# Two more slots for converted weights, the last three inner blocks taken output by output, and the operand differences of the second MLP moved

## The chip, the cores and the metric

The kernel runs on one core of one Trainium2 chip. The metric is the device time of one execution in microseconds. The engines of the core are named as in the profile: PE (TensorE, matmuls; PEld is its weight load), DVE (VectorE), ACT (ScalarE), POOL (GpSimd) and SP (SyncE, which issues the DMAs here).

## The reference

Attention, then two MLPs on 1152 tokens (2 batches of 576) with 512 features. The parts that the change touches are the two MLPs:

```python
def _moe_ref(x, w_in, w_out):                 # first MLP: 512 -> 2048 -> 512
    h = x @ w_in
    relu6 = np.clip(h + 3.0, 0.0, 6.0)
    g = h * relu6 / 6.0
    return g @ w_out

def _moe2_ref(x, domain_probs, w1, w2):       # second MLP: 4 experts, 512 -> 1024 -> 512
    p = domain_probs / (domain_probs.sum(-1, keepdims=True) + 1e-09)
    out = 0
    for e in range(4):
        h = np.maximum(x @ w1[e], 0.0)
        out += p[:, e:e + 1] * (h @ w2[e])
    return out
```

## The kernel before

All matmuls of the MLPs are three-term products: each float32 operand is a high part, which TensorE takes as it is, and a low part (the difference), and high x high, high x low and low x high are accumulated (`three`, L350, and `product`, L861). ACT makes a high part by a copy, DVE the low part by a subtraction.

**First MLP.** The weights come as 16 pieces of 128 x 1024 double-precision words: 8 of `w_in`, then 8 of `w_out`. The generator `converting` (L173) turns a piece into a high and a low half in steps: DVE masks (L219), DVE adds the low word (L229) and ACT prepares the next piece's scale (L195), DVE multiplies (L241, L250) and ACT copies the high half (L203), DVE subtracts the low half (L208). `convert(n)` takes n steps if more than two slots are free; `need` takes as many as are needed. A piece uses a slot for its source (`raw`), one for scratch (`temps`) and keeps one for the result. Slots of 8 KiB per partition come from pools: `slots` (11), `mlp1` (6) and, once the attention's result x is no longer needed, `more` (4), which lies where x was. The function `take` goes through a list of pools in order and takes the first that has a slot by the count kept while the program is written out.

The first product, `first` (L763), runs for 16 inner blocks f of 128 and 3 token groups c of 384; its result, gated, goes to `gate_of` slots, five blocks to a slot. The second product, `second` (L834), runs c by c, f by f: `split_gate` makes the pair h (high by ACT L787, low by DVE L788) two blocks ahead, and each h is multiplied with four pieces of weight, one for each of four outputs dt of 128 features, 12 matmuls in all (L354 to L356), accumulating in four PSUM banks. After f = 15 ACT evicts the four outputs to x2 (L853). The tile `h` has NF2 = 8 buffers. The order of TensorE is that of the program. DVE, ACT and POOL are ordered by a planner in this part, which simulates the program and lets an engine take, of what is ready, what stands first in the program.

**Second MLP.** The tokens are two halves (s = 0 and 1) of 576. The products follow a scheme that works on differences of blocks: `blocks_of_x2(s, xop)` takes the four blocks b[c, h] (c: features, h: half of the tokens) of x2, makes four differences on POOL (L278, called by `sub2`), and splits seven operands, named 11, T2, T1, T3, 21, 22, T4, each by an ACT copy (L284) and a DVE subtraction (L289). It is a generator, and one step is one operand. For s = 0 it runs during the last token group of the first MLP (`prepare_first`, two steps per block), with w1 and w2 of the first expert (`load_in`, `sum_in`, `prepare_in`, `prepare_out`; the four sums of a w1 part are on POOL, L407 and L278). For s = 1 it runs after the last token group. From there on DVE, ACT and POOL follow the program's order too. A round r has four `Unit2` of 42 products: `open` (12), `middle` (18) and `close` (12), with a unit's close after the next one's open. Close accumulates into the banks of middle, once DVE has read them (L407). Then nine token tiles go through `second2` (L1098 to L1100).

In round 0 two operands of s = 1 are split ahead of unit 1, three after it, and the rest after unit 2. The shares `pr` of the experts (L1120 to L1125) are computed before all that.

Of the kernel before, what the change touches and what calls it, by code (L numbers as in the profile page):

```python
# [80 lines left out]
NB = 6  # L81
NX = 2 * KD * NT // SLOT

# [27 lines left out]
def model(ctx: ExitStack, tc: tile.TileContext, qT, kT, v, dp, w_in, w_out, w1, w2, out):  # L114
# [45 lines left out]
    sources = [w_in[i].bitcast(I32) for i in range(NW)] + [w_out[i].bitcast(I32) for i in range(NW)]  # L160
    raw, wt = {}, {}
    loaded = [0]
    SHORT = ("more", "slots", "mlp1")
    LONG, FIRST = ("mlp1", "slots"), ("slots", "mlp1")

    def load_to(n):
        while loaded[0] <= min(n, len(sources) - 1):
# [109 lines left out]
    def sub2(out, a, b, eng=None):  # L277
        (eng or nc.gpsimd).tensor_tensor(out=out, in0=a, in1=b, op=ALU.subtract)  # L278
# [503 lines left out]
        )  # L782

    def split_gate(c, f):
        g = hp_.tile([P, 2, TC], F32R, tag="h", name="h", bufs=NF2)
        u = gate_of(c, f)
        nc.scalar.activation(out=g[:, 0, :], in_=u, func=AF.Copy)  # L787
        nc.vector.tensor_tensor(out=g[:, 1, :], in0=u, in1=r32(g[:, 0, :]), op=ALU.subtract)  # L788
        n = c * NF1 + f
        if n % PER == PER - 1 or n == NTC * NF1 - 1:  # L790
            give(g_slots.pop(n // PER))
        return g
# [14 lines left out]
    def blocks_of_x2(s, x):  # L807

        b = {}
        for c in (0, 1):  # L810
            t = x2_pair(s, c)[:, : 2 * PAIR].rearrange("p (k a n) -> p k a n", k=2, a=2)
            for h in (0, 1):
                b[c, h] = t[:, :, h]
        room = x2_pair(s, 0)[:, 2 * PAIR : 3 * PAIR].rearrange("p (k n) -> p k n", k=2)
        x = x.rearrange("p (b h k n) -> p b h k n", b=7, h=2, k=2)

        def put(at, of):
            return splits([(x[:, at, 0], x[:, at, 1], of)])

        yield from put(0, b[0, 0])  # L820
        sub2(b[0, 0], b[0, 1], b[0, 0])
        sub2(room, b[1, 1], b[0, 0])
        sub2(b[0, 1], b[1, 1], b[0, 1])
        yield from put(4, b[1, 0])
        sub2(b[1, 0], b[1, 0], room)
        yield from put(1, room)
        yield from put(2, b[0, 0])
        yield from put(3, b[0, 1])
        yield from put(5, b[1, 1])
        yield from put(6, b[1, 0])  # L830
        for c in (0, 1):
            give(x2_slots.pop((s, c)))

    def second(c, f, g, accs):  # L834
        n = NW + f // 2
        need(n)
        for dt in range(KD):
            c0 = (f % 2) * DM + dt * P
            three(
                accs[dt],  # L840
                wt[n],
                slice(c0, c0 + P),
                (g[:, 0, :], g[:, 1, :]),
                f == 0,
                f == NF1 - 1,
            )
        if f < NF1 - 1:
            return
        for dt in range(KD):
            for s, n0 in enumerate((0, PAIR)):  # L850
                lo, hi = max(c * TC, n0), min((c + 1) * TC, n0 + PAIR)
                if lo < hi:
                    nc.scalar.activation(  # L853
                        out=x2_at(s, dt)[:, lo - n0 : hi - n0],
                        in_=accs[dt][:, lo - c * TC : hi - c * TC],
                        func=AF.Copy,
                        scale=1.0 / UP**2,
                    )


    def product(ps, a, b, start, stop):  # L861
# [150 lines left out]
    psum.pop("pair").release()  # L1012
    psum["many"] = ctx.enter_context(tc.tile_pool(name="many", bufs=6, space=PSUM))
    att.release()
    hp_ = tc.alloc_tile_pool(name="hp", bufs=1, side="right")
    for f in range(NF1):
        for c in range(1 if f < EARLY else 0, NTC):
# [33 lines left out]
    for n, (c, f) in enumerate(gs):  # L1051
        if f == 0:
            accs = [bank(TC) for _ in range(KD)]
        if n + 2 < len(gs):
            ready.append(split_gate(*gs[n + 2]))
        second(c, f, ready.pop(0), accs)
        if c == 0:
            convert(2, 1)
        elif c == 1 and f == 3:
            for _ in conv:  # L1060
                pass
        elif c == 2 and f == 0:
            assert unused.pop("more") == NX
            pools.pop("more").release()
            work["sums"] = ctx.enter_context(
                tc.tile_pool(name="sums", bufs=1, reuse_waits="tile")
            )
            xops.append(work["sums"].tile([P, 28 * TB], F32R, name="xop0"))
            first_of = prepare_first()
        elif c == 2:  # L1070
            run(first_of, 2)
        if c == NTC - 1 and f % 2:
            done_with(NW + f // 2)
    assert unused.pop("mlp1") == NB
    for _ in first_of:
        pass
    hp_.release()
    pools.pop("mlp1").release()
    work["pool"] = tc.alloc_tile_pool(name="work", bufs=1, side="right", reuse_waits="tile")
    xops.append(work["pool"].tile([P, 28 * TB], F32R, name="xop1"))  # L1080
# [10 lines left out]
    def second2(r, t, h):  # L1091
# [24 lines left out]
    )  # L1116
    dps = work["pool"].tile([P, NTT, E], F32, name="dps")
    nc.sync.dma_start(out=dps, in_=dp)
    psum_ = work["pool"].tile([P, NTT], F32, name="psum_")
    nc.vector.tensor_reduce(out=psum_, in_=dps, op=ALU.add, axis=AX.X)  # L1120
    nc.vector.tensor_scalar(out=psum_, in0=psum_, scalar1=1e-9, scalar2=None, op0=ALU.add)
    prec = work["pool"].tile([P, NTT], F32, name="prec")
    nc.vector.reciprocal(out=prec, in_=psum_)
    pr = work["pool"].tile([P, NTT, E], F32, name="pr")
    nc.vector.tensor_tensor(  # L1125
        out=pr, in0=dps, in1=prec.unsqueeze(2).to_broadcast([P, NTT, E]), op=ALU.mult
    )
    load_in(1)
    for r in range(NR):
        h = [  # L1130
            work["pool"].tile([P, 2, 2, NT], F32R, tag="h", name="h", bufs=2) for _ in range(2)
        ]
        if r == 0:
            order, steps = [(0, 0), (1, 0), (0, 1), (1, 1)], blocks_of_x2(1, xops[1])
        else:
            order, steps = [(0, 0), (0, 1), (1, 0), (1, 1)], prepare_out(r, 1)
            load_in(r + 1)
        before = None
        run(steps, 2 if r == 0 else 0)
        for i, (n, p) in enumerate(order):  # L1140
            unit = Unit2(r, n, xops[p], h[n], p)
            unit.open()
            if before:
                before.close()
            unit.middle(before)
            before = unit
            run(steps, 3 if r == 0 else 1)
            if i == 1:
                for _ in steps:
                    pass  # L1150
                load_out(r + 1)
            if i == 2:
                sum_in(r + 1, 0)
        for t in range(NTT):
            second2(r, t, h)
            if t == 0:
                before.close()
                before.lows()
                for n in (0, 1):
                    drop(w_in2, (r, n))  # L1160
                steps = chain(prepare_in(r + 1, 0), prepare_in(r + 1, 1), prepare_out(r + 1, 0))
            run(steps, 2 if t % 2 else 1)
        for _ in steps:
            pass
        for q in (0, 1):
            drop(w_out2, (r, q))
# [46 lines left out]
```

## Time and profile before

| | us |
|---|---|
| median of 3 runs | 665.03 (663.31 to 666.17) |
| the profiled execution | 664.96 |
| its span, first to last instruction | 663.1 |
| PE busy | 646.5 (97%) |
| DVE busy | 419.1 (63%) |
| ACT busy | 251.7 (38%) |
| POOL busy | 102.3 (15%) |

The granted TensorE clock is 0.995 of full speed over the span. In the trace the first product of the first MLP ends near 175.5 us, its second product runs from there to 279.1, the second MLP (eight rounds) from there to the end. Each row of a timeline gives start and duration in us, engine, line, operation, what is written and read, and in brackets the idle time before it and what ended that. Consecutive rows of one line are merged ("x4"), with their union as the duration.

### The profile page before, as it was taken

How to read it: one execution, taken by the hardware profiler on the slowest of the kernel's cores; microseconds unless marked ns; L12 is line 12 of the kernel's file. 1: busy time of each engine (PE TensorE's matmuls, PEld its weight loads, DVE VectorE, ACT ScalarE, POOL GpSimd, SP SyncE). 2: the span in 40 equal slices, each digit the busy share in tenths (PEclk: the TensorE clock that was granted, in tenths of full speed). 3: DMA queues.
4: the chain of work that ended last, by engine and by line, in shares of the span. 5: the costliest groups of instructions: out<-in, count | busy, mean ns of one | idle time of the engine just before them, and what ended most of it. 6: DMA issues, size and time to landing. Idle time of an engine off the chain costs nothing.

```text
span 663.1 us, 11940 instructions
## 1 busy us (share of the span) xinstructions
PE 646.5 (97%) x4930; PEld 582.3 (88%) x4943; DVE 419.1 (63%) x825; ACT 251.7 (38%) x588; POOL 102.3 (15%) x146
## 2 busy tenths in 40 slices
PE   6989999999999999989999999999999999999997
PEld 3556899999998999988898898998998998988985
DVE  7466799942598229296575575665665665665742
ACT  2556666542475236243142232233232241331310
POOL 4653100000000035060120211201201201201000
PEclk8989999999999999999999999999999999999999
DMA  8933313300350013200120110110110210300012
GB/s 264 341 90 128 124 64 127 127 1 0 127 192 1 0 64 92 100 1 2 48 81 0 64 65 1 63 64 1 65 64 0 73 56 0 127 2 1 1 48 96
DMA packets 11860, 45.89 MB, mean 69 GB/s; under 512 B 1303, under 2 KB 3351, under 8 KB 7709
## 3 DMA queue, kind: packets, MB, share of 16 engines
q1 hardware_dynamic: 11804, 45.12, 20.1%
q8 instruction: 39, 0.64, 0.4%
q14 instruction: 17, 0.13, 0.1%
HBM read 42.76 MB, written 2.36 MB: 68 GB/s over the span
## 4 chain that ended last, share of the span: by engine, by line
PE 89%; DVE 8%; issue 1%; ACT 1%; POOL 0%; POOLq 0%; ACTq 0%
PE bank L865 25%; PE bank L1098 10%; PE bank L1100 10%; PE bank L1099 10%; PE bank L356 9%; PE bank L354 9%; PE bank L355 8%; PE pair L514 2%; PE pair L707 2%; DVE slot L229 1%; PE pair L428 1%; DVE slot L208 1%; PE pair L718 1%; DVE slot L250 1%; PE pair L687 1%
## 5 line engine op out<-in xcount | busy, mean ns | idle before, releaser
L865 PEld LDWEIGHTS bank<-xop,slot 128*128 128x128 f32 x1344 | 180.8, 188 | 3.8 <-DVE u L407 2.5
L865 PE MATMUL bank<-xop,slot 128*128 128x288 f32 x1344 | 182.1, 295 | 2.0 <-DVE u L407 2.0
L1098 PE MATMUL bank<-slot,h 128*128 128x512 f32 x288 | 113.4, 394 | 0.0
L1100 PE MATMUL bank<-slot,h 128*128 128x512 f32 x288 | 113.0, 392 | 0.0
L1099 PE MATMUL bank<-slot,h 128*128 128x512 f32 x288 | 111.9, 389 | 0.0
L1106 DVE SCALAR_TENSOR_TENSOR slot<-bank,pr,slot 128x512 f32<-128x512 f32 x63 | 47.3, 751 | 82.5 <-PE bank L1100 82.5
L407 POOL TENSOR_TENSOR st<-slot 128x256 f32<-128x256 f32 x16 | 13.2, 825 | 443.1 <-DMA slot<-in_w_dram 223.2
L356 PE MATMUL bank<-h,slot 128*128 128x384 f32 x192 | 65.0, 338 | 0.9 <-DVE slot L208 0.9
L354 PE MATMUL bank<-h,slot 128*128 128x384 f32 x192 | 64.8, 338 | 0.5 <-ACT slot L203 0.5
L1100 PEld LDWEIGHTS bank<-slot,h 128*128 128x128 f32 x288 | 54.1, 188 | 12.6
L355 PE MATMUL bank<-h,slot 128*128 128x384 f32 x192 | 64.6, 337 | 0.0
L1099 PEld LDWEIGHTS bank<-slot,h 128*128 128x128 f32 x288 | 54.1, 188 | 11.5
L1098 PEld LDWEIGHTS bank<-slot,h 128*128 128x128 f32 x288 | 54.1, 188 | 10.3
L354 PE MATMUL bank<-x,slot 128*128 128x384 f32 x188 | 63.1, 336 | 0.0
L356 PE MATMUL bank<-x,slot 128*128 128x384 f32 x188 | 62.9, 335 | 0.0
L355 PE MATMUL bank<-x,slot 128*128 128x384 f32 x188 | 62.9, 335 | 0.0
L407 DVE TENSOR_TENSOR u<-bank,u 128x288 f32<-128x288 f32 x96 | 43.6, 454 | 20.8 <-PE bank L865 20.5
L894 ACT ACTIVATE h<-c 128x288 fp32r<-128x288 f32 x64 | 27.9, 445 | 72.5 <-DVE c L407 72.5
L780 DVE SCALAR_TENSOR_TENSOR slot<-t,bank 128x384 f32<-128x384 f32 x47 | 25.8, 552 | 28.7 <-ACT t L779 28.4
L779 ACT ACTIVATE t<-bank,half__171 128x384 f32<-128x384 f32 x47 | 27.1, 581 | 41.9 <-PE bank L356 41.9
L284 ACT ACTIVATE slot<-st 128x512 fp32r<-128x512 f32 x32 | 19.2, 624 | 62.2 <-POOL st L278 62.2
L788 DVE TENSOR_TENSOR h<-slot,h 128x384 fp32r<-128x384 f32 x48 | 27.6, 584 | 22.2 <-ACT h L787 22.2
(113 smaller groups left out, 929.9 us busy)
## 6 DMA issues: line engine op xcount, KB each, us to landing
slot<-in_w_dram SPq DMA_DIRECT2D x16, 1024.0 KB, 4.8
slot<-in_w_in_dram SPq DMA_DIRECT2D x8, 1024.0 KB, 5.5
slot<-in_w_out_dram SPq DMA_DIRECT2D x8, 1024.0 KB, 4.8
slot<-in_v_dram SPq DMA_DIRECT2D x6, 512.0 KB, 9.1
out_dram<-slot SPq DMA_DIRECT2D x9, 256.0 KB, 2.0
slot<-in_kT_dram SPq DMA_DIRECT2D x3, 576.0 KB, 6.7
slot<-in_qT_dram SPq DMA_DIRECT2D x6, 288.0 KB, 6.1
slot<-in_kT_dram SPq DMA_DIRECT2D x2, 288.0 KB, 3.7
```

The source lines that it names most:

```text
L354: nc.tensor.matmul(ps, wh, xh, start=first, stop=False)
L355: nc.tensor.matmul(ps, wh, xl, start=False, stop=False)
L356: nc.tensor.matmul(ps, wl, xh, start=False, stop=last)
L407: eng.tensor_tensor(out=out, in0=a, in1=b, op=ALU.add)
L779: nc.scalar.activation(out=t, in_=ps, func=AF.Relu, bias=half_, scale=1.0 / (6.0 * UP))
L788: nc.vector.tensor_tensor(out=g[:, 1, :], in0=u, in1=r32(g[:, 0, :]), op=ALU.subtract)
L865: nc.tensor.matmul(ps, a[:, i, k], b[:, j, k], start=start and k == 0 and n == 0, stop=stop and k == 1 and n == 2, skip_group_check=True,)
L894: nc.scalar.activation(out=self.h[:, 0, i, j], in_=of, func=AF.Relu)
L1098: nc.tensor.matmul(ps, hh, w[:, 0], start=(f == 0), stop=False)
L1099: nc.tensor.matmul(ps, hh, w[:, 1], start=False, stop=False)
L1100: nc.tensor.matmul(ps, hl, w[:, 0], start=False, stop=(f == NF - 1))
L1106: nc.vector.scalar_tensor_tensor(out=to, in0=ps, scalar=share, in1=to, op0=ALU.mult, op1=ALU.add)
```

## The change

- A pool `late` of NL = 2 slots is opened when the attention's room is free, next to `h`, whose buffers go from 8 to NH = 4. The lists of `take` name it: sources, scratch and first gated blocks may go there, later weights and loads prefer it.
- In the last token group, the last LAST = 3 inner blocks are multiplied output by output: for each dt the nine matmuls of f = 13, 14 and 15, then its eviction (`put_x2`).
- `blocks_of_x2` starts with three of the four differences, into places of their own (t1, t2) so that none of them overwrites a block that is still to be split, and the order of the operands is 11, 21, 22, T1, T2, T3, T4.
- In round 0, three operands are split ahead of unit 1, then one after each open and one after each middle of units 1 and 2. The shares are computed after unit 2 (`shares`).

```diff
+NL = 2
+NH = 4
+LAST = 3
-    SHORT = ("more", "slots", "mlp1")
-    LONG, FIRST = ("mlp1", "slots"), ("slots", "mlp1")
+    SHORT = ("more", "slots", "late", "mlp1")
+    LONG, FIRST = ("late", "mlp1", "slots"), ("slots", "late", "mlp1")
...
-        g = hp_.tile([P, 2, TC], F32R, tag="h", name="h", bufs=NF2)
+        g = hp_.tile([P, 2, TC], F32R, tag="h", name="h", bufs=NH)
...
-        yield from put(0, b[0, 0])
-        sub2(b[0, 0], b[0, 1], b[0, 0])
-        sub2(room, b[1, 1], b[0, 0])
-        sub2(b[0, 1], b[1, 1], b[0, 1])
-        yield from put(4, b[1, 0])
-        sub2(b[1, 0], b[1, 0], room)
-        yield from put(1, room)
-        yield from put(2, b[0, 0])
-        yield from put(3, b[0, 1])
-        yield from put(5, b[1, 1])
+        sub2(t1, b[0, 1], b[0, 0])
+        sub2(t2, b[1, 1], t1)
+        sub2(b[0, 1], b[1, 1], b[0, 1])
+        yield from put(0, b[0, 0])
+        yield from put(4, b[1, 0])
+        sub2(b[1, 0], b[1, 0], t2)
+        yield from put(5, b[1, 1])
+        yield from put(2, t1)
+        yield from put(1, t2)
+        yield from put(3, b[0, 1])
         yield from put(6, b[1, 0])
...
-    def second(c, f, g, accs):
+    def second(c, fs, gs, accs):
+        for f in fs:
+            need(NW + f // 2)
         for dt in range(KD):
+            for f, g in zip(fs, gs):
+                c0 = (f % 2) * DM + dt * P
+                three(accs[dt], wt[NW + f // 2], ...)
+            if f == NF1 - 1:
+                put_x2(c, dt, accs[dt])
...
+    pools["late"] = tc.alloc_tile_pool(name="late", bufs=NL, side="right")
+    unused["late"] = NL
...
-        second(c, f, ready.pop(0), accs)
+        if c < NTC - 1 or f < NF1 - LAST:
+            second(c, [f], [ready.pop(0)], accs)
+        elif f == NF1 - LAST:
+            second(c, range(f, NF1), ready, accs)
...
-        run(steps, 2 if r == 0 else 0)
+        run(steps, 3 if r == 0 else 0)
         for i, (n, p) in enumerate(order):
             unit = Unit2(r, n, xops[p], h[n], p)
             unit.open()
+            if r == 0:
+                run(steps, 1)
             if before:
                 before.close()
             unit.middle(before)
             before = unit
-            run(steps, 3 if r == 0 else 1)
+            run(steps, 1)
+            if r == 0 and i == 1:
+                shares()
```

## Rows read from the trace of the kernel before

**Rows 1.** The page, part 4: shares of the span in the chain that ended last

```profile
PE 89%; DVE 8%; issue 1%; ACT 1%; POOL 0%; POOLq 0%; ACTq 0%
```

**Rows 2.** Timeline of PE around the two late weights: start, duration, instruction, [idle before]

```profile
200.77 0.34 PE L356 MATMUL bank<-h,slot 128*128 128x384 f32 x1
202.76 0.33 PE L354 MATMUL bank<-h,slot 128*128 128x384 f32 x1
...
206.23 0.34 PE L356 MATMUL bank<-h,slot 128*128 128x384 f32 x1
...
207.84 0.44 PE L356 MATMUL bank<-h,slot 128*128 128x384 f32 x1 [0.39 <-DVE slot L208]
208.12 0.34 PE L354 MATMUL bank<-h,slot 128*128 128x384 f32 x1
```

**Rows 3.** Windows: stretch, length, busy us of each engine, clock, DMA share, GB/s

```profile
144.00:175.00 31.00, 31.00 (x180) 31.00 (x180) 8.61 (x16) 8.73 (x15) 0.00 (x0) 1.00 0.00 1
175.50:195.00 19.50, 19.50 (x113) 19.50 (x112) 19.31 (x35) 13.89 (x26) 0.00 (x0) 1.00 0.70 248
195.00:208.80 13.80, 12.39 (x65) 10.81 (x64) 13.80 (x27) 7.34 (x14) 0.00 (x0) 1.00 0.08 32
269.00:279.00 10.00, 10.00 (x59) 10.00 (x58) 0.00 (x0) 1.18 (x3) 0.00 (x0) 1.00 0.28 96
```

**Rows 4.** Timeline of DVE: the first conversion step after the first product

```profile
175.59 0.69 DVE L219 TENSOR_SCALAR slot<-slot 128x1024 int32<-128x1024 int32 x1 [0.91 <-PE bank L356]
```

**Rows 5.** Timeline of PE at the seam of the MLPs

```profile
279.14 11.45 PE L865 MATMUL bank<-xop,slot 128*128 128x288 f32 x84
292.11 1.06 PE L865 MATMUL bank<-xop,slot 128*128 128x288 f32 x6 [1.52 <-DVE u L407]
293.66 9.06 PE L865 MATMUL bank<-xop,slot 128*128 128x288 f32 x66 [0.49 <-DVE u L407]
```

**Rows 6.** Chain that ended last, in order of time: start, step, what

```profile
204.24 0.47 DVE h L788
...
329.06 20.78 PE bank L865 x156
```

**Rows 7.** Timeline of ACT, DVE and POOL at the seam

```profile
277.75 2.08 ACT L853 ACTIVATE slot<-bank 128x384 f32<-128x384 f32 x4 [10.96 <-PE bank L356]
279.73 1.25 ACT L284 ACTIVATE xop<-slot 128x576 fp32r<-128x576 f32 x2
...
281.02 1.42 DVE L289 TENSOR_TENSOR xop<-slot,xop 128x576 fp32r<-128x576 f32 x2
...
286.00 4.60 DVE L289 TENSOR_TENSOR xop<-slot,xop 128x576 fp32r<-128x576 f32 x3 [0.44 <-ACT xop L284]
...
290.88 0.80 DVE L407 TENSOR_TENSOR c<-bank,u 128x288 f32<-128x288 f32 x2
...
281.85 6.91 POOL L278 TENSOR_TENSOR slot<-slot 128x576 f32<-128x576 f32 x4 [19.48 <-DVE xop L289]
```

**Rows 8.** Timeline of ACT: one h in the steady second product

```profile
218.27 0.52 ACT L787 ACTIVATE h<-slot 128x384 fp32r<-128x384 f32 x1 [1.57 <-PE bank L356]
```

**Rows 9.** Timeline of POOL and of DVE as the third token group begins

```profile
242.41 0.74 POOL L407 TENSOR_TENSOR st<-slot 128x256 f32<-128x256 f32 x1 [172.21 <-DMA slot<-in_w_dram]
...
245.51 1.42 POOL L278 TENSOR_TENSOR slot<-slot 128x576 f32<-128x576 f32 x1
248.01 5.52 POOL L278 TENSOR_TENSOR slot<-slot 128x576 f32<-128x576 f32 x3 [1.08 <-ACT slot L853]
...
244.02 0.93 DVE L788 TENSOR_TENSOR h<-slot,h 128x384 fp32r<-128x384 f32 x1 [1.56 <-ACT h L787]
247.69 0.76 DVE L289 TENSOR_TENSOR xop<-slot,xop 128x576 fp32r<-128x576 f32 x1 [2.73 <-ACT xop L284]
248.70 6.35 DVE L289 TENSOR_TENSOR xop<-slot,xop 128x576 fp32r<-128x576 f32 x4 [0.26 <-ACT xop L284]
254.97 0.55 DVE L788 TENSOR_TENSOR h<-slot,h 128x384 fp32r<-128x384 f32 x1
```

More of the change, by code (lines that the diff above doesn't have):

```diff
@@ L813, in blocks_of_x2 @@
                 b[c, h] = t[:, :, h]
-        room = x2_pair(s, 0)[:, 2 * PAIR : 3 * PAIR].rearrange("p (k n) -> p k n", k=2)
+        t1, t2 = (
+            x2_pair(s, c)[:, 2 * PAIR : 3 * PAIR].rearrange("p (k n) -> p k n", k=2) for c in (0, 1)
+        )
         x = x.rearrange("p (b h k n) -> p b h k n", b=7, h=2, k=2)
@@ L832, in blocks_of_x2, with put_x2 @@
             give(x2_slots.pop((s, c)))
-    def second(c, f, g, accs):
-        n = NW + f // 2
-        need(n)
+    def second(c, fs, gs, accs):
+        for f in fs:
+            need(NW + f // 2)
         for dt in range(KD):
[L838 to L858, printed above, removed]
+            for f, g in zip(fs, gs):
+                c0 = (f % 2) * DM + dt * P
+                three(
+                    accs[dt],
+                    wt[NW + f // 2],
+                    slice(c0, c0 + P),
+                    (g[:, 0, :], g[:, 1, :]),
+                    f == 0,
+                    f == NF1 - 1,
+                )
+            if f == NF1 - 1:
+                put_x2(c, dt, accs[dt])
+    def put_x2(c, dt, acc):
+        for s, n0 in enumerate((0, PAIR)):
+            lo, hi = max(c * TC, n0), min((c + 1) * TC, n0 + PAIR)
+            if lo < hi:
+                nc.scalar.activation(
+                    out=x2_at(s, dt)[:, lo - n0 : hi - n0],
+                    in_=acc[:, lo - c * TC : hi - c * TC],
+                    func=AF.Copy,
+                    scale=1.0 / UP**2,
+                )
     def product(ps, a, b, start, stop):
@@ L1077, in model @@
     hp_.release()
+    assert unused.pop("late") == NL
+    pools.pop("late").release()
     pools.pop("mlp1").release()
@@ L1118, in model, with shares @@
     nc.sync.dma_start(out=dps, in_=dp)
[L1119 to L1123, printed above, removed]
-    pr = work["pool"].tile([P, NTT, E], F32, name="pr")
-    nc.vector.tensor_tensor(
-        out=pr, in0=dps, in1=prec.unsqueeze(2).to_broadcast([P, NTT, E]), op=ALU.mult
-    )
+    pr = work["pool"].tile([P, NTT, E], F32, name="pr")
+    def shares():
+        psum_ = work["pool"].tile([P, NTT], F32, name="psum_")
+        nc.vector.tensor_reduce(out=psum_, in_=dps, op=ALU.add, axis=AX.X)
+        nc.vector.tensor_scalar(out=psum_, in0=psum_, scalar1=1e-9, scalar2=None, op0=ALU.add)
+        prec = work["pool"].tile([P, NTT], F32, name="prec")
+        nc.vector.reciprocal(out=prec, in_=psum_)
+        nc.vector.tensor_tensor(
+            out=pr, in0=dps, in1=prec.unsqueeze(2).to_broadcast([P, NTT, E]), op=ALU.mult
+        )
     load_in(1)
```

## The prediction

> **What bounds the kernel now.** The chain of work that ended last is TensorE for 89% of the span [rows 1]. A gain can therefore come only from places where TensorE waits. I looked for them by the spacing of its matmuls between 80 and 330 us. There are two places.
>
> *The second product of the first MLP, near 200 us.* Matmuls follow each other at 0.173 us (113 in 19.50 us, rows 3). From 200.77 to 202.76 four steps take 1.99 us, and from 206.23 to 208.12 they take 1.89 us: 1.3 + 1.2 = **2.5 us** lost, and the matmul at 207.84 waits for DVE L208, the low half of a converted weight [rows 2]. The windows show why: from 144 to 175 us DVE is busy 8.61 of 31.00 us, and from 175.5 to 208.8 it is busy 19.31 + 13.80 = 33.1 of 33.3 us [rows 3]. DVE did not convert in the idle stretch because the next weight's scratch lies in the pool that reuses the room of x: its first instruction, L219 at 175.59, waited for TensorE's last read of x [rows 4].
>
> *The seam between the MLPs.* The 84 products from 279.14 run freely, then TensorE waits 1.52 and 0.49 us for DVE's additions L407; the last ends at 293.66 + 9.06 = 302.72. That is 23.6 us for 156 products, which take 20.8 us (20.9 with the last one's tail) in later rounds [rows 5, 6]: **2.6 us** lost. DVE was late there because three subtractions L289 took 4.60 us, 1.53 each, while GpSimd ran four of 6.91 us; two with GpSimd mostly idle took 1.42 us, 0.71 each [rows 7].
>
> So everything to win is 5.1 us of 664.96, the profiled execution's own time; the median of the runs is 665.03, so sums on the one hold for the other.
>
> **1. Two more slots.** By the order of takes and gives, two gated-value blocks move into the new pool, and scratch and source of one more weight (the eleventh) land in slots that exist before x is released. One whole weight is then converted between 144 and 175 us, where DVE is idle 22 us and TensorE busy for 31.00 of 31.00 [rows 3]. A weight costs (33.1 - 13 x 0.47) / 6 = 4.5 us of DVE (six weights, twelve h low halves and one gate in the stretch; 0.47 from rows 6). Against that, four h halves that were made early now fall into the stretch: 4 x 0.47 = 1.9 us. DVE ends 2.6 us earlier, against a last lateness of 1.2 us and a sum of 2.5. Bounds: nothing gained, if the planner puts the saved time elsewhere, or all 2.5. I take 2.2, because both late places are shorter than the shift.
>
> **2. Four h buffers instead of eight.** This is the room that pays for the slots. A block takes 1.57 + 0.52 = 2.1 us, and ScalarE starts an h when TensorE frees a buffer [rows 8]. An h takes 0.52 + 0.55 us [rows 8, 9], so it is ready 7 x 2.1 - 1.1 = 13.6 us ahead of its use with eight, and 3 x 2.1 - 1.1 = 5.2 us with four. One stretch uses more than that: after the low half at 244.02 DVE makes none until 254.97, while it makes operand differences at 1.59 us each (6.35 / 4) against GpSimd's at 1.84 (5.52 / 3; 1.42 alone) [rows 9]. The third token group starts 16 x 2.1 before 279.14, at 245.5; with four buffers its blocks 3, 4 and 5 want an h at 251.8, 253.9 and 256.0. Were the order kept, block 3's would be done at 254.97 + 0.55 = 255.5: **3.7 us lost**. The planner goes by program order among what is ready, and blocks 3 and 4 have their h ahead of most differences there, so I expect first difference, h, two differences, h, two differences, h. A second thing lengthens it: the load of the first w1 part waits for a slot that an h sets free, and GpSimd began on it, released by that DMA, at 242.41 [rows 9]. With four buffers that h is made four blocks later, so the sums begin at 242.4 + 8.4 = 250.8 or after; the four of them (0.74 each alone) then follow the differences instead of leading them, and hold DVE up again. From 247.69, when DVE begins on the first: 0.8 + 1.4 + 1.6 + 1.6 + 1.4 ends block 4's h at 254.5, 0.6 late; two differences and an h against sums, 1.4 + 1.4 + 1.2, end at 258.5, another 1.9 late (an h beside GpSimd is put at 1.59 less the 0.2 that it is shorter, anything beside a sum at its own time and 0.7). With fewer meetings it is 0.5 to 1. Ends 0 and 3.7; I take **1.8 lost**, between the two walks.
>
> **3. Last three blocks output by output.** The same 36 matmuls. The first output ends three outputs x 9 matmuls = 4.7 us before the end instead of 1.6, the last as before. The three h must be there within 1.1 us of the chunk's start; the last takes the buffer that block 11 frees, 2.1 us before, and needs 1.1. DVE stands idle then (0.00 us from 269 to 279, rows 3). No cost; if h were late there, its lateness is the price.
>
> **4. The differences at the seam.** Call 279.14 zero. Evictions take 2.08 / 4 = 0.52 each, and the last ends at 0.7 [rows 7], also in the new order. GpSimd's first difference now needs only the first two outputs and is done at about -1.0. The second starts at 0.7 and holds to 2.1. ScalarE's copies, 1.25 for two, let DVE want its first subtraction at 1.3, held until 2.1, done 2.7 (0.6 once it is let go, an estimate from 0.71 alone). The second, behind GpSimd's third, is done a pair later: 2.7 + 1.84 = 4.6. The third follows at once, 5.2, since GpSimd's fourth needs the second's read; the addition of unit 1 (0.40, rows 7) ends 5.6. The fourth subtraction waits for GpSimd until 6.6 and ends 7.2, and the next addition, which frees the bank that unit 1's close accumulates into, ends 7.6. TensorE is there after 42 products x 0.133 = 5.6 [rows 5, 6]: it waits **2.1 us**. Before, unit 1's close did not wait. The next such place is reached at 13.3, with its addition done near 12.7. The four small share operations move behind and free 0.6 us (the first copy ends near 279.73 + 0.7, the first subtraction starts at 281.02). So 2.6 becomes 2.1: gain 0.5. Bounds: 0 lost without meetings (1.3 + 4 x 0.7 + 2 x 0.4 = 4.9, under 5.6), and 3.6 lost if the second close waits 1.5 again.
>
> What a meeting of the two engines costs I took as a mean of rows: 0.71 alone, 1.53 to 1.59 beside GpSimd [rows 7, 9]. The worst that rows allow is a whole GpSimd difference and the own time each time, 1.42 + 0.7 = 2.1; with that for all four the seam would lose 1.3 + 4 x 2.1 + 0.8 - 5.6 = 4.9 us. The Trainium skill (SBUF — State Buffer, Who interferes with whom) speaks for that worst case and against this placement: a VectorE instruction with two SBUF inputs and a GpSimd one that reads SBUF shut each other out, and the later one waits for the whole of the other. The means in the rows agree with it if DVE comes on average part way into GpSimd's instruction.
>
> **Sum.** -2.2 + 1.8 - 0.5 = -0.9: **664.0 us**.
>
> **Rivals.** *B, the h stay ahead:* the planner places them so that the fewer buffers cost nothing; -2.2 - 0.5 gives 662.2, and 661.2 with shares of the rest. For it: program order; against it: 10 us without an h before. *C, both places filled:* no meetings at the seam either, 664.96 - 5.1 = 659.9. Against it: GpSimd and DVE now start together. *D, starved of h:* the differences stay in one run ahead of the h, 3.7 lost, seam as before: -2.2 + 3.7 gives 666.5, slower. It decides from the point where DVE's gap between two h exceeds 5.2 us; 10 us today speak for it. A part of D is the full exclusion in every meeting: 4.9 instead of 2.6 at the seam and 1.8 for the h, -2.2 + 1.8 + 2.3 gives 666.9. *E, the conversions do not move:* 1.8 - 0.5 gives 666.3; against it, DVE's long idle time and the wait on x's room.
>
> **Chances.** Forecast 0.40 (662.9 to 665.2), B 0.22, C 0.10, D 0.20 (0.05 of it the full exclusion), E 0.08. The range 660.3 to 667.2 leaves out most of C and D's far end. A measurement of this kernel tells about 0.5%, 3.3 us, from no change. Below 661.7 lie C, half of B and a little of the forecast: 0.24. Above 668.3 lies only a D whose two losses add up: 0.04. The rest is 0.72.
>
> **What would show it.** Step 1: ten DVE groups L219 become eleven before x's last read, and the gaps near 201 and 207 us are gone. Step 2: matmuls L354 that wait for DVE L788 between 251 and 260 us; none of them is B, over 3 us is D. Step 4: L865 waiting for L407 after 42 products rather than 84; evictions spread over 5 us. A TensorE wait in the first product, or a planner's order with fewer h ahead of the conversions, would make all of this wrong.

## The result and the profile after

The changed kernel takes **671.38 us** (median of 4 runs, 670.25 to 672.25) where the kernel before takes 664.48 beside it: a ratio of 1.0098, with a 95% interval of 1.0071 to 1.0125. It is slower by 6.9 us; forecast were 664.0, within 660.3 to 667.2.

The profiled executions have spans of 663.1 and 670.5 us. The start of each kind of TensorE's matmuls cuts them into stages:

| stage | before, us | after, us | difference | forecast |
|---|---|---|---|---|
| until the first MLP's first product | 75.19 | 75.81 | +0.6 | 0 |
| its first product | 100.20 | 100.18 | 0.0 | 0 |
| its second product | 103.75 | 106.96 | +3.2 | -0.4 |
| seam: 156 products | 23.42 | 23.15 | -0.3 | -0.5 |
| the rounds after it, to the last matmul | 355.94 | 359.66 | +3.7 | 0 |
| after the last matmul | 4.64 | 4.77 | +0.1 | 0 |

The first line is no work of the change: in the runs below, whose attention is the same, it lies anywhere from 72.8 to 79.5 us. So the kernels are compared stage by stage, which agree within some 0.4 us between executions of the same work where the clock doesn't fall, rather than by single times. Two stages hold the loss, and one of them the forecast didn't touch at all. Below, a wait "by spacing" is the time from one matmul's start to the next less the usual step between them.

**Second product, the gain.** The windows that answer [rows 3] (stretch, length, busy us of PE, PEld, DVE, ACT, POOL, clock, DMA share, GB/s):

```profile
144.00:175.00 31.00, 31.00 (x181) 31.00 (x180) 10.97 (x21) 9.77 (x17) 0.00 (x0) 1.00 0.00 1
175.50:195.00 19.50, 19.50 (x113) 19.50 (x112) 18.69 (x34) 12.28 (x24) 0.00 (x0) 1.00 0.60 217
195.00:208.80 13.80, 13.80 (x81) 13.80 (x80) 12.04 (x23) 7.51 (x14) 0.00 (x0) 1.00 0.00 0
```

DVE does 2.4 us more while it was idle (10.97 for 8.61) and 2.4 less in the two stretches behind (30.7 for 33.1). TensorE is busy for all of the third stretch: the gaps of [rows 2] are gone.

**Second product, the loss.** The only matmuls of it that wait, by the timeline of PE (start, duration, [idle before and what ended it]):

```profile
252.41 0.44 PE L360 MATMUL bank<-h,slot 128*128 128x384 f32 x1 [0.33 <-DVE h L793]
...
255.83 0.44 PE L360 MATMUL bank<-h,slot 128*128 128x384 f32 x1 [1.05 <-DVE h L793]
...
263.84 0.45 PE L359 MATMUL bank<-h,slot 128*128 128x384 f32 x1 [1.64 <-ACT h L792]
264.62 0.44 PE L360 MATMUL bank<-h,slot 128*128 128x384 f32 x1 [0.34 <-DVE h L793]
```

By the spacing of the matmuls (0.174 us is the pace) these cost 0.6, 1.3 and, both together, 2.5 us: **4.4 us**. The chain that ended last shows what stood behind them; for 20 us it leaves TensorE (start, step, what):

```profile
245.92 1.61 DVE h L793
247.53 3.81 DVE xop L294 x2
251.34 1.02 DVE h L793
252.36 2.42 DVE xop L294 x2
254.78 1.00 DVE h L793
255.77 1.61 DVE slot L291 x4
...
261.98 0.74 POOL st L283
262.74 0.64 ACT slot L289
...
264.10 0.48 DVE h L793
264.62 0.44 PE bank L360
```

First h, two differences, h, two differences, h, on DVE; then GpSimd's second four sums of the first expert's weights, ScalarE's copy of a sum, and h behind that. GpSimd's timeline shows what it had waited for before these sums:

```profile
258.59 1.92 POOL L412 TENSOR_TENSOR st<-slot 128x256 f32<-128x256 f32 x1 [3.24 <-DVE slot L294]
```

The sums have one buffer, `st` (`bufs=1`), and DVE was reading the first four sums out of it until then. Right behind the last wait the clock falls (windows as above):

```profile
264.00:266.00 2.00, 1.66 (x7) 1.39 (x8) 1.03 (x3) 0.43 (x2) 0.00 (x0) 0.80 0.99 414
266.00:268.00 2.00, 2.00 (x8) 2.00 (x7) 1.56 (x3) 2.00 (x5) 0.00 (x0) 0.50 0.17 70
268.00:270.00 2.00, 2.00 (x12) 2.00 (x11) 2.00 (x5) 1.21 (x3) 0.00 (x0) 0.85 0.00 0
```

Ten matmuls from 265.29 to 268.49 follow each other at 0.32 us, the 1.2 GHz level, instead of 0.174: 1.5 us more. The stage adds up: 103.75 - 2.7 + 4.4 + 1.5 = 106.95, and 106.96 was measured. The 2.7 are the two gaps of [rows 2], 2.5 by spacing, and a smaller stop of 0.25 us in the kernel before, between the matmuls at 196.68 and 197.28, which the prediction had not counted.

**Seam.** Timelines of PE and of DVE, which answer [rows 5] and [rows 7]:

```profile
282.95 5.75 PE L874 MATMUL bank<-xop,slot 128*128 128x288 f32 x42
290.71 15.56 PE L874 MATMUL bank<-xop,slot 128*128 128x288 f32 x114 [2.00 <-DVE u L412]
...
284.25 4.16 DVE L294 TENSOR_TENSOR xop<-slot,xop 128x576 fp32r<-128x576 f32 x3 [8.46 <-ACT xop L289]
288.33 0.44 DVE L412 TENSOR_TENSOR u<-bank,u 128x288 f32<-128x288 f32 x1
288.70 1.59 DVE L294 TENSOR_TENSOR xop<-slot,xop 128x576 fp32r<-128x576 f32 x1
290.21 1.00 DVE L412 TENSOR_TENSOR u<-bank,u 128x288 f32<-128x288 f32 x2
```

One wait instead of two, after 42 products instead of 84.

**Rounds.** The 96 matmuls in a row of the second MLP's second products, from the first to the product that follows them, in the kernel before and after:

```profile
306.90 0.39 PE L1098 MATMUL bank<-slot,h 128*128 128x512 f32 x1
...
328.89 1.35 PE L865 MATMUL bank<-xop,slot 128*128 128x288 f32 x9
```

```profile
310.50 0.39 PE L1114 MATMUL bank<-slot,h 128*128 128x512 f32 x1
...
332.89 1.36 PE L874 MATMUL bank<-xop,slot 128*128 128x288 f32 x9
```

They take 21.99 us before and 22.39 after, without a wait in either: 229.0 and 233.3 ns per matmul. There are 108 of them in a round and eight rounds, and all 864 together take 3.4 us more. The other 0.3 us of the stage's 3.7 are in the products with 288 columns, which go from 133.1 to 133.4 ns.

### The profile page after: what moved, and what is told of

Same layout as the page of the kernel before. It is cut to its first block, busy times and chain, and to the rows that moved or that the text cites. A ratio compares the mean times of both kernels' runs of the same rounds, so it can differ in the third digit from the quotient of the medians.

```text
span 670.5 us, 11971 instructions
## 1 busy us (share of the span) xinstructions
PE 654.8 (98%) x4943; PEld 584.5 (87%) x4943; DVE 419.7 (63%) x825; ACT 251.4 (37%) x588; POOL 104.1 (16%) x146
## 4 chain that ended last, share of the span: by engine, by line
PE 59%; DVE 3%; POOL 1%; ACT 0%; issue 0%; POOLq 0%
PE bank L874 26%; PE bank L1116 10%; PE bank L1115 10%; PE bank L1114 10%; DVE xop L294 2%; PE bank L360 1%; PE bank L361 1%; PE bank L359 1%; DVE h L793 1%; POOL st L283 0%; POOL st L412 0%; DVE slot L291 0%; ACT xop L289 0%; DVE slot L294 0%; DVE u L412 0%
## 5 line engine op out<-in xcount | busy, mean ns | idle before, releaser
L412 POOL TENSOR_TENSOR st<-slot 128x256 f32<-128x256 f32 x16 | 14.9, 928 | 274.7 <-DVE slot L294 197.1
L283 POOL TENSOR_TENSOR slot<-slot 128x576 f32<-128x576 f32 x8 | 13.3, 1682 | 193.6 <-ACT slot L862 191.7
```

The source lines that it names most:

```text
L412: eng.tensor_tensor(out=out, in0=a, in1=b, op=ALU.add)
```

## The experiments

Two theories were to be tested: **place**, that the rounds are slower because the change moved a tile in SBUF, and **depth**, that the waits for h come from four buffers. The change allocates two small tiles (the shares' sums and reciprocals, 128 bytes together) inside a function that is called after the second MLP's h tiles are allocated, and so h lies 128 bytes lower: at 352 modulo 512 instead of 480 (the remainder of its byte address in a partition, divided by 512). h is the stationary operand of these matmuls, the one that is loaded as weights; the moving one lies in `slots`, at 32 modulo 512. Times are medians; the stages are those of each run's trace.

**x1: the tiles put back in place.** Edit of the changed kernel:

```diff
+    psum_ = work["pool"].tile([P, NTT], F32, name="psum_")
+    prec = work["pool"].tile([P, NTT], F32, name="prec")
     pr = work["pool"].tile([P, NTT, E], F32, name="pr")
     def shares():
-        psum_ = work["pool"].tile([P, NTT], F32, name="psum_")
...
-        prec = work["pool"].tile([P, NTT], F32, name="prec")
```

> The changed kernel, with the two small tiles of the shares (sums, reciprocals) allocated ahead of the shares again; their instructions stay where the change put them. That moves the second MLP's h tiles back by 128 bytes, to where they lay in the kernel before, and touches nothing else. Theory place (the second MLP's second products are slower because of where their stationary operand lies in SBUF): the 864 matmuls of those products go from 233.3 ns back to 229 ns each, 3.6 us in all, and the time from 671.4 to 667.8 us. Rival order (they are slower because the engines beside them work in another order, or because the granted clock of that execution was 0.990 instead of 0.995): they stay at 233 ns or vary with the clock, and the time stays at 671.4.

Measured: 667.48 us beside 665.20 of the kernel before (as for x2 to x4), ratio 1.0038 [1.0003, 1.0074]; the rounds take 355.94 us, as before the change:

```profile
307.38 0.39 PE L1114 MATMUL bank<-slot,h 128*128 128x512 f32 x1
...
329.37 1.88 PE L874 MATMUL bank<-xop,slot 128*128 128x288 f32 x13
```

21.99 us for the 96. The waits for h stay as they were, within 0.02 us (1.65 and 0.34 at the last). No half clock (the 1.2 GHz level) follows them here (second product 105.4 us); it comes behind the seam's wait instead, with 0.92, 0.50 and 0.73 granted from 286 to 292 us, and makes that stage 24.6. *Place* holds; that single executions differ by where the clock falls is seen on the way.

**x2: the kernel before, with its tile moved.**

```diff
+    pr = work["pool"].tile([P, NTT, E], F32, name="pr")
+    h0 = [
+        work["pool"].tile([P, 2, 2, NT], F32R, tag="h", name="h", bufs=2) for _ in range(2)
+    ]
     psum_ = work["pool"].tile([P, NTT], F32, name="psum_")
...
-        h = [
+        h = h0 if r == 0 else [
```

> The kernel before, with the first round's h tiles allocated ahead of the two small tiles of the shares: the second MLP's h tiles lie 128 bytes lower, as in the changed kernel; every instruction and its place is as before. Theory place: the second products' matmuls go from 229 to 233.3 ns, and the time from 664.5 to 668.1 us. Rival order: no change, 664.5.

Measured: 669.29 us, ratio 1.0056 [1.0019, 1.0094]; rounds 359.66 us, and 22.39 for the 96:

```profile
310.17 0.39 PE L1098 MATMUL bank<-slot,h 128*128 128x512 f32 x1
...
332.56 1.63 PE L865 MATMUL bank<-xop,slot 128*128 128x288 f32 x11
```

Every other instruction is as before. Place alone makes the 3.7 us, whichever kernel has it.

**x3: parts 3 and 4 alone**, **x4: parts 1 and 2 alone.** x3 is x1 with `NH = 8` and without the pool of two slots; x4 is the kernel before with the two slots and `bufs=4` for h.

> The changed kernel with the h tiles of the second MLP put back, without the two slots and with eight buffers for h: of the change, the last three blocks by output and the new order of the operand differences remain. Theory depth (the waits for h near 252, 254 and 262 us, 4.5 us, and the ten matmuls at half clock behind them, 1.5 us, come from four buffers instead of eight): they vanish, the two waits for late converted weights near 200 and 207 us, 2.7 us, come back, the seam has one wait of 2.1 us after 42 products; first MLP's second product 103.7 us, seam 23.1, time 664.2 us. Rival differences (the waits for h come from the new order of the differences, whatever the buffers): 4 to 6 us of waits stay near 252 to 268 us, and the time is 668 to 670.

> The kernel before with the two slots and four buffers for h; order of the differences, of the last blocks and the places of the second MLP's tiles as before. Theory depth: no wait near 200 and 207 us (2.7 us less), but waits for h between 250 and 270 us of 4.5 us or more, with a stretch at half clock behind: 664.5 - 2.7 + 6.0 = 667.8 us. Rival differences: no or little wait for h, 664.5 - 2.7 = 661.8 us.

Measured: x3 666.11 us (1.0010 [0.9978, 1.0042]), second product 103.98, no wait for h, the gaps of the late weights back, seam 23.14. x4 667.59 us (1.0039 [1.0007, 1.0072]), second product 105.42, with the same waits for h as x1, and seam 23.72, as before within the spread of that stage. So the new order of the differences and of the last blocks neither makes nor cures a wait for h, and the half clock isn't always part of it.

**z1: the depth alone.** The kernel before with one number:

```diff
-        g = hp_.tile([P, 2, TC], F32R, tag="h", name="h", bufs=NF2)
+        g = hp_.tile([P, 2, TC], F32R, tag="h", name="h", bufs=4)
```

> The kernel before with four h buffers instead of eight: one number. Theory depth: the waits for h between 249 and 266 us come back as in the run with the two slots and four buffers, 4.5 us in all (0.6, 1.3 and 2.5), and the waits for late converted weights near 200 and 207 us stay as in the kernel before, 2.7 us; the first MLP's second product takes 103.75 + 4.5 = 108.2 us where no stretch at half clock follows, and the seam and the rounds stay as before. Rival slots (what made h late was the earlier conversion, or the blocks moved into the two slots, and not the number of buffers): less than 1 us of waits for h, 103.75 to 104.5 us.

Measured (one execution, as for all runs below but the last two): second product 111.2 us, 3 more than expected. The waits for h, the timeline of PE:

```profile
255.37 0.44 PE L355 MATMUL bank<-h,slot 128*128 128x384 f32 x1 [0.24 <-DVE h L788]
258.78 0.44 PE L355 MATMUL bank<-h,slot 128*128 128x384 f32 x1 [1.03 <-DVE h L788]
266.82 0.44 PE L354 MATMUL bank<-h,slot 128*128 128x384 f32 x1 [1.62 <-ACT h L787]
267.60 0.44 PE L355 MATMUL bank<-h,slot 128*128 128x384 f32 x1 [0.34 <-DVE h L788]
```

4.3 us by spacing: *depth* holds, for the buffers alone. The rest: the waits for late weights grow from 2.7 to 4.5 us; when the second product starts, four low halves of h have been made instead of eight, and the other four now compete with the conversions (the prediction put them at 4 x 0.47 = 1.9). And 1.5 us of half clock follow (0.59 and 0.56 granted from 268 to 272).

**y1: early conversion without new room.** The kernel before with the guard of the conversions eased in the first product's loop:

```diff
             first(c, f)
-            convert(1)
+            convert(1, 2 if f < NF1 - 2 else 0)
```

> The kernel before with one edit in the loop of the first MLP's first product: from f = 14 on, when no block of gated values is left to be given a slot, conversions go on as long as any slot is unused, where they stopped at two. By the order of takes and gives the scratch and the source of the eleventh weight then land in slots that exist before x is released, as with the two new slots, and all eight h buffers stay. Theory: the waits for late converted weights come from the order of takes, not from a lack of room; they are gone (2.7 us), no wait for h appears, the second product takes 103.75 - 2.7 = 101.0 us and the execution 664.5 - 2.7 = 661.8. Rival: the slots come free too late (weight 6 is read until some 13 us before the first product ends), so DVE gains no idle time and 1 to 2.7 us of the waits stay.

Measured: 662.19 us in its one execution, 665.44 the kernel before beside it; second product 101.28 us, no matmul of it waits. Windows as above:

```profile
144.00:174.50 30.50, 30.50 (x178) 30.50 (x176) 12.76 (x23) 10.63 (x19) 0.00 (x0) 1.00 0.00 1
174.90:208.00 33.10, 33.10 (x190) 33.10 (x189) 30.69 (x56) 20.07 (x38) 0.00 (x0) 1.00 0.36 128
```

The same shift as in the changed kernel, 2.4 us out of the full stretch, with all eight buffers. The room that the change paid for with h buffers was there: once the last block of gated values has its slot, nothing needs the two slots that the guard kept.

**d5: five buffers**, on top of y1.

> The run with conversions going on to the last unused slot, with five h buffers instead of eight. Theory lead: h is ready (n - 1) x 2.1 - 1.1 us ahead of its use with n buffers, 5.2 with four; with four the waits for h added up to 4.4 us, so the stretch wants 5.2 + 4.4 = 9.6 us of lead, and five buffers, which give 7.3, leave 2.3 us of waits for h: second product 101.3 + 2.3 = 103.6 us, six would leave 0.2. Rival throughput (DVE can't make the h in that stretch whatever the lead): 4 us or more stay, 105.3 us or more. Rival threshold (with one buffer more the planner's order comes out right): no wait, 101.3 us.

```profile
263.76 0.44 PE L354 MATMUL bank<-h,slot 128*128 128x384 f32 x1 [1.40 <-ACT h L787]
264.54 0.45 PE L355 MATMUL bank<-h,slot 128*128 128x384 f32 x1 [0.35 <-DVE h L788]
```

The first two waits are gone, the third is left: 2.3 us by spacing, as *lead* says. The stage takes 105.0 us and not 103.6, because a stretch at half clock follows again (0.92, 0.50, 0.72 from 264 to 270), 1.5 us by spacing.

**w1 and w2: what makes h late.** Both from x1. w1 leaves out GpSimd's second four sums, w2 its four operand differences of the first half of the tokens.

```diff
+        if (r, n) == (0, 1):
+            sums_of[r, n] = kept[0]
+            return
```

```diff
-        sub2(t1, b[0, 1], b[0, 0])
-        sub2(t2, b[1, 1], t1)
-        sub2(b[0, 1], b[1, 1], b[0, 1])
+        if s:
+            sub2(t1, b[0, 1], b[0, 0])
...
+        else:
+            t1, t2 = b[0, 1], b[1, 1]
```

> The run with the changed kernel and the h tiles of the second MLP put back, without GpSimd's four sums of the second half of the first expert's weights (the sums of the first half are used again): the output is not the reference's. In that run the third wait for h, 2.5 us, came while ScalarE stood 4.2 us at a copy of those sums with two copies of h behind it in its queue. Theory queue: without the sums ScalarE does not stand there, the third wait (2.5 us) is gone, the first two (0.6 and 1.3 us) stay; second product 105.4 - 2.5 = 102.9 us. Rival load (DVE and ScalarE are simply too busy in that stretch, and h would be late there in any order): 1.5 us or more of the third wait stays, 104.4 us or more.

> The same run without GpSimd's four operand differences of the first half (T1 to T4 are made from undifferenced blocks; the output is not the reference's); DVE's seven subtractions there stay. Theory meetings: the first two waits for h, 0.6 and 1.3 us, come from DVE subtractions that took 1.6 to 2.0 us beside GpSimd's differences instead of 0.7; without them the two are gone or under 0.3 us together, and the third, which hangs on the sums, stays or shrinks as the sums begin earlier; second product 105.4 - 1.9 = 103.5 us or less. Rival order (what delays these h is that two differences stand ahead of each in DVE's queue, at whatever duration): 1 us or more of the first two waits stays.

w1: second product 103.44 us. The waits of PE:

```profile
249.67 0.44 PE L365 MATMUL bank<-h,slot 128*128 128x384 f32 x1 [0.33 <-DVE h L798]
253.09 0.44 PE L365 MATMUL bank<-h,slot 128*128 128x384 f32 x1 [1.05 <-DVE h L798]
...
257.84 0.44 PE L365 MATMUL bank<-h,slot 128*128 128x384 f32 x1 [0.28 <-DVE h L798]
```

The first two are untouched. The third, 2.5 us at the ninth block of the token group, is gone, and one of 0.6 at the eighth stands in its place: 2.0 us net came from ScalarE standing at the copy of a sum. *Queue* holds, with a small rest of *load*. w2: second product 101.04 us, and no wait for h at all. DVE there:

```profile
242.42 0.56 DVE L793 TENSOR_TENSOR h<-slot,h 128x384 fp32r<-128x384 f32 x1 [0.54 <-ACT h L792]
242.99 1.43 DVE L294 TENSOR_TENSOR xop<-slot,xop 128x576 fp32r<-128x576 f32 x2
```

The order of DVE's queue is the same, h and two differences; they take 0.72 each instead of 1.9. So the differences on GpSimd start all of it: beside them DVE's take more than twice as long, and without them the same order of work leaves no wait, against rival *order*. The third wait goes too. But w2 also frees GpSimd of the four differences themselves, 6.8 us in x1, and the sums begin at 245.3 us instead of 247.8; whether the third wait would go with the meetings alone is not shown.

**s1: a scan of the place.** The kernel before, with h at another offset in a wider tile in each of the eight rounds:

```diff
+        at = (0, 8, 16, 24, 32, 48, 64, 96)[r]
+        h = [
+            w[:, at : at + 4 * NT].rearrange("p (a f n) -> p a f n", a=2, f=2) for w in wide
+        ]
```

> The kernel before with the second MLP's h tiles 512 bytes wider, and in each of the eight rounds h laid at another offset in them: 0, 32, 64, 96, 128, 192, 256 and 384 bytes. So the address of h in round 1 to 8 is 480, 0, 32, 64, 96, 160, 224 and 352 modulo 512; the other operand's slots stay. Theory place: the step of the second products' matmuls depends on that residue alone: 229.0 ns in the first round, 233.3 ns in the last, and other values between, perhaps below 229, in the rest. Rival: the two paces belong to the two layouts as a whole (what else was moved, or the distance of the two h tiles); then the rounds differ by less than 0.5 ns, or the last round doesn't show 233.3.

First of the 96 and the product behind them, in rounds 2 and 3:

```profile
353.13 0.40 PE L1098 MATMUL bank<-slot,h 128*128 128x512 f32 x1
...
375.52 0.29 PE L865 MATMUL bank<-xop,slot 128*128 128x288 f32 x1
...
400.68 0.40 PE L1098 MATMUL bank<-slot,h 128*128 128x512 f32 x1
...
422.45 0.29 PE L865 MATMUL bank<-xop,slot 128*128 128x288 f32 x1
```

22.39 and 21.77 us, where round 1 has 21.99. All eight rounds, mean step of the 96:

| h at, modulo 512 | 480 | 0 | 32 | 64 | 96 | 160 | 224 | 352 |
|---|---|---|---|---|---|---|---|---|
| ns | 229.0 | 233.4 | 226.8 | 233.2 | 233.3 | 233.3 | 229.0 | 233.3 |

*Place* holds, within one execution. Three levels; addresses 256 bytes apart (224 and 480, 96 and 352) give the same one, and the shortest step is at 32, where the slots of the other operand lie too.

**y2: the seam spread.** x3 with one low half (11's) ahead of the first unit's additions on DVE, instead of three or four, and the others behind them; the low halves of 21 and 22 go to GpSimd.

> The run with the seam alone, with the second half's operand differences spread further: only the low half of 11 stands ahead of the first unit's additions on DVE; the low halves of 21 and 22 are made by GpSimd; T2's comes behind the first unit's middle, T1's and T3's behind the second's, T4's behind the third's. Theory queue (TensorE waits 2.16 us after 42 products because three or four subtractions of operands stand ahead of the additions of the first unit on DVE): the first unit's last addition is done near 4.1 us after the seam instead of 7.7, the wait is gone, and the seam takes 23.1 - 2.1 = 21.0 us. Rival load (DVE has too much to do in the seam in any order): the wait moves to a later place, after 84 or 126 products, and the seam takes 22 to 23.5 us.

Measured: 660.07 us in its one execution; seam 21.41 us, and the wait after 42 products is gone:

```profile
276.69 13.09 PE L920 MATMUL bank<-xop,slot 128*128 128x288 f32 x97
290.07 8.20 PE L920 MATMUL bank<-xop,slot 128*128 128x288 f32 x59 [0.29 <-DVE xop L283]
```

The first unit's last addition is done at 4.4 us after the seam (4.1 expected). *Queue* holds, and a wait of 0.45 us is left, at the operand T1, as *load* says on a smaller scale.

**f1 and f2: together.** f1 is y2 with y1's guard, T1's low half on GpSimd too, and the second MLP's h at 32 modulo 512; f2 reserves 448 bytes at the edge of SBUF instead of behind h, so that the first MLP's h and the converted weights on that side come to 32 as well.

```diff
+    work["pool"].tile([P, 16], F32, name="gap")
...
+    edge = ctx.enter_context(tc.tile_pool(name="edge", bufs=1, side="right"))
+    edge.tile([P, 112], F32, name="gap3")
```

> What the runs so far gave, together: eight h buffers and no new slots, conversions going on to the last unused slot from f = 14 on, the last three blocks output by output, the second half's operand differences spread over the seam with three of the low halves on GpSimd (T1's now too, ahead of 22's), and the second MLP's h tiles at 32 modulo 512 as the slots are (64 bytes between the shares and h, 448 behind h so that the operands' place stays). From the kernel before: waits for converted weights -2.5 (101.3), seam 23.4 to 20.9, 864 matmuls from 229.0 to 226.8 ns -1.9; 664.5 - 2.5 - 2.5 - 1.9 = 657.6 us, a ratio of 0.990. Rival: the gains don't add up, because a later place takes over in the seam (21.4 or more) or conversions and differences meet again; 659 to 661.

> The same, with 448 bytes reserved at the edge of SBUF instead of behind h: everything that is allocated from that side moves down by 448 bytes, so that the first MLP's h tiles and the converted weights on that side lie at 32 modulo 512 as well, like the slots. Theory residue (the step is shortest where both operands of a matmul have the same address modulo 256): the second product of the first MLP, which mixes operands at 480 and 32 and now has 175.4 ns per matmul, goes to 173.5; 576 x 1.9 = 1.1 us less than the run beside it, 656.5. Rival: the pace of the products with h as the moving operand doesn't go by that; no change, 657.6, or more where the attention's tiles, moved too, become slower.

| | kernel before | f1 | f2 |
|---|---|---|---|
| median, us | 664.36 | 658.58 | 657.50 |
| ratio, 95% interval | | 0.9918 [0.9886, 0.9951] | 0.9903 [0.9877, 0.9929] |
| second product of the first MLP, us | 103.75 | 101.28 | 99.84 |
| seam, us | 23.42 | 21.97 | 21.96 |
| rounds, us | 355.94 | 354.39 | 354.39 |

Both beat both kernels. In the seam the expectation of 20.9 was wrong: T1's low half is in time now, and TensorE waits 0.6 us for T3's instead, from DVE, 103 products in, and stops 0.2 us twice more; that part of the rival came true. The seam is even 0.6 us longer than in y2, so moving T1's low half gained nothing.

In f2 the second product's step goes from a mean of 175.8 ns to 173.3, so *residue* holds for the first MLP also. f1 shows the same inside one execution: its h lies at 480 modulo 512, its converted weights at 480 or, in `slots`, at 32. The 24 matmuls from the first line on have weights at 480, the 48 from the second line on weights at 32:

```profile
183.97 0.34 PE L359 MATMUL bank<-h,slot 128*128 128x384 f32 x1
...
188.14 0.34 PE L359 MATMUL bank<-h,slot 128*128 128x384 f32 x1
...
196.62 0.33 PE L359 MATMUL bank<-h,slot 128*128 128x384 f32 x1
```

That is 173.5 ns per matmul, then 176.6, and so it goes on to the end of the stage. The medians of f1 and f2 don't tell the two apart; this stage does.

The page of f2 (part 4, shares of the chain that ended last) against [rows 1]:

```profile
PE 96%; DVE 2%; issue 0%; ACT 0%; ACTq 0%
```

## Why the prediction was wrong, step by step

**Step 1, two more slots: right.** 2.7 us of waits gone where 2.2 was taken and 2.5 was the bound, which missed the small stop near 197 us. Eleven conversions begin before x's last read instead of ten, as foretold, the eleventh at 141.9 us; DVE's shift was 2.4 us where 2.6 was worked out.

**Step 2, four h buffers: the order right, the walk too short, 1.8 us where 4.4 were measured.** The planner's order came as foretold (one difference, h, two, h, two, h), and the sums began at 250.69 where 250.8 was worked out. The walk gave 0.6 and another 1.9 us late and was then cut to 1.8 in all; measured were 0.6, 1.3 and a third of 2.5. The first two make 1.9, so the 1.8 was near what it stood for. What failed is this:

- The walk stopped too soon. It ended at the sixth block's h and followed DVE's queue and not ScalarE's. There two copies of h stood behind a copy of a sum, which came 4.2 us after ScalarE was free, because GpSimd had waited for DVE to empty `st`: 2.5 us, of which w1 shows 2.0 to be that queue. The prediction had no term for it.
- The half clock had no term either. In the profiled execution of the changed kernel, in x1, z1, d5 and w1 a stretch at the 1.2 GHz level follows one of the waits, some 1.5 us by spacing in each, and in x4 none. Which wait it follows differs between executions of the same order of work; what decides that stays open.

The prices inside the walk were off both ways and cancelled, which is luck. It put two differences and an h at 1.6 + 1.6 + 1.4 beside GpSimd's differences, and at 1.4 + 1.4 + 1.2 beside its sums. Measured were 1.9 each and 1.0 in the first case, 1.2 each and 1.0 in the second; the h ahead of both took 1.6 where 1.4 was put. GpSimd's three differences, by its timeline in the changed kernel, took 1.78 each where one alone takes 1.42 [rows 9]:

```profile
245.39 5.34 POOL L283 TENSOR_TENSOR slot<-slot 128x576 f32<-128x576 f32 x3 [1.07 <-issue]
```

So where the two engines run in step, 1.9 is nearer to the prediction's worst case of 2.1, a whole instruction of the other engine each time, than to its mean of 1.6, and w2 shows 0.72 without GpSimd. The prediction had priced that worst case for the seam and not for the h. The Trainium skill (SBUF — State Buffer, Who interferes with whom) says that an instruction of DVE with two SBUF inputs and one of GpSimd that reads SBUF contend for shared ports, which only one of them holds at a time. The trace comes near the 2.1 that a whole wait each time would give, and doesn't reach it. The same section says that an instruction of DVE with at most one SBUF input, outside its 2-port modes, doesn't contend, and the seam agrees: the addition at 288.33, which reads PSUM and SBUF, took 0.44 beside a difference of GpSimd.

**Step 3, the last three blocks: right.** No matmul waits from 269 us to the seam, in the changed kernel or in x3.

**Step 4, the seam: right.** 2.16 us lost after 42 products, forecast 2.1; the later place doesn't wait. The gain is 0.3 us instead of 0.5; the seams of the runs with the old order lie between 23.4 and 23.8 us, so its size is known to some 0.4 us only. The cause was as worked out (y2), and so was its cure within reach: the operands weren't too many, but too many stood ahead of the additions.

**The step that was not there.** The prediction began with the premise that time is to be won, and so lost, only where TensorE waits. The four operations of the shares were counted as 0.6 us of DVE that moves away. That their two tiles are allocated at another point, and that what is allocated behind them moves by 128 bytes, was in the diff and had no term: 3.7 us, half of the loss, without a wait. f1 and f2 win 1.5 us and another 1.4 in the same way.

Without the 3.7 the changed kernel's 671.4 would be 667.7 (x1 measured 667.5), still 0.5 us above the range; without the half clock, if the median execution has it as the profiled one does, 666.2. So it takes the place and the stops that the walk left out to explain a time outside the range. 666.2 lies next to rival D's 666.5, but that is a coincidence: the waits for h add up to 4.4 us, over the 3 us that were D's sign, yet D's order, all differences ahead of the h, did not come.

## What to carry to other kernels

When a diff moves an allocation, write down where every tile behind it lies before and after: here 128 bytes changed the pace of 864 matmuls, and no wait in any view shows it; only the spacing of matmuls that wait for nothing does. A buffer's depth is worth the lead that its stretch uses at its worst (9.6 us here by d5's sum, which its measurement fits, against 5.2 with four buffers), and a walk through the queues has to follow each in-order queue through which the buffer is filled, and go on until the lateness is gone. Before room is bought, see which guard keeps room unused.

## What the runs showed of the hardware

The step of a 512-column matmul went from 226.8 to 229.0 or 233.4 ns with nothing but the address of its stationary operand, and was the same at addresses 256 bytes apart in the two pairs tried; with 384 columns and the first MLP's h as the moving operand it was 173.3 to 173.5 where both lie at the same address modulo 512, and 176.6 where the weights lie at 32 and h at 480 (f1). The Trainium skill (TensorE: Matmul & The Clock Gate, Step-by-step: what each phase is for) says that TensorE has two independent read ports to SBUF and that loading the next weights takes no bandwidth from the running matmul. These steps differ by up to 3% with the addresses of the two operands, and the section speaks of no such dependence. That equal addresses are fastest doesn't hold for all products either: the first MLP's first product has 173.4 to 173.5 in every run, though its weights lie at 32 or 480 and x at 32. What in the chip makes the levels, no run here shows.

After a wait of 2 us or so TensorE's granted clock fell to 0.50, the 1.2 GHz level, for some 3 us in five executions, and not in others with the same wait (x3, w2 and the changed kernel, all 2.16 us at the seam; x4, with x1's waits for h).
